# Two more activation tiles turned by transposed transfers, and the rows of the first block in another order

## The chip, the cores and the metric

The kernel runs on one core of a Trainium2 chip. The metric is device time in microseconds (us) of one execution; less is better. The core has five engines that run side by side, each with its own stream of instructions: TensorE (matrix products, and transposes by a product with the identity), VectorE (elementwise work and reductions), ScalarE (activations, copies out of the accumulators), GpSimd (POOL in the profile) and SyncE (SP), which mostly sends transfers between the device's memory and the on-chip buffer. A stream is worked off in order, and an instruction that waits holds everything behind it on its engine. Transfers of all queues are carried by the same sixteen DMA engines. Matrix products write to eight accumulator banks, which another engine has to empty.

## The reference

The reference computes a sum of three terms and all of its gradients: the input itself, a sequence branch A (short convolution, then a long convolution done through Fourier transforms, gated by the normed input) and a gated MLP, branch B. Only the MLP and the norm matter here. Sequence length S is 2048, width D 1024, hidden width F 3584; all in bf16.

```python
xn = _layernorm(x)                       # rows of D
gate = einsum("bsd,df->bsf", xn, W_gate)
up   = einsum("bsd,df->bsf", xn, W_up)
gate = gate * (gate > 0)
h = gate * up
out = x + A(xn, ...) + einsum("bsf,fd->bsd", h, W_down)
```

The gradient of h needs `grad_out` times `W_down` transposed, for the same rows and the same columns of F as gate and up. It is computed in the same pass.

## The kernel before

The sequence is cut into 16 tiles ("rows" below) of 128; a half is 8 rows. F is cut into 7 blocks of 512 columns. `hidden` (class `LnMlp`) runs over 14 steps: for each half, for each block. A step has its weights on chip: `wg` and `wu` (gate and up, 1024 x 512 each, in four transfers of 256 KB) and `wdT` (the down weights turned, four transposed transfers). For each of its 8 rows it does three products of eight 128 x 512 matmuls: `gate(s)`, `up(s)` (both with the turned activations `xnT` of the row) and `grad_row(s)` (with the turned output gradient `goT` of the row). ScalarE empties gate and gradient rows, VectorE masks and multiplies; the results go to device memory as `h_d` and `ug_d`.

The first step (`n == 0`, `ahead` in the code) is special, since nothing is on chip when the kernel starts. Its rows are normed while it runs. `layer_norm` is a generator: each `next(ln)`, or `chunk()`, which calls it up to three times, emits one more piece: sums on ScalarE, small steps on VectorE, the scaling by 1/std (line 991), which makes a tile ready. The input arrives in loads: load 4 holds tiles 4 and 5, load 5 tiles 6 and 7, later loads the rest.

`flip_xn(st)` (line 1131) turns a normed tile into `xnT`. For tiles 0 to 5 TensorE does it: eight 128 x 128 transposes into an accumulator bank (line 1141), then a copy out by VectorE, for tile 4 by ScalarE (line 1146). For tiles 6 and 7 SyncE sends a transposed transfer from the tile on chip (line 1134), without TensorE.

The order on TensorE in the first step is: rows 0 to 3 of gate and up, interleaved with the turning of tiles 0 to 3 (`first_rows`); gradient rows 0 and 1, with the turning of tiles 4 and 5 within row 1 (`grad(0)`, which calls `flip_ahead`); gate rows 4, 5, up rows 4, 5 (`gate_up(4)`); gradient rows 2, 3, 4, 5; gate rows 6, 7, up rows 6, 7; gradient rows 6, 7. Then the second step (`n == 1`) begins, with gate rows 0 and 1.

The order of transfers on SyncE's queue follows the program's order and priorities. `load_T` (line 1122) sends a turned gradient tile, `col_block` (line 1091) the gate or up weights of a step, `row_piece_T` (line 1116) a quarter of the down weights, `ln_load` (line 943) a load of the input. `issue_after(ins)` makes what is emitted inside it be placed after `ins`. A transfer takes one of eight completion semaphores in turn, and waits for the transfer that had it before. The gate weights of the second step go to a spare buffer; its up and down weights go to buffers that the first step's gate row 7 and up row 7 free. POOL's queue stores `h_d` and `ug_d` in the first step, and the normed tiles `xn_d`.

Of the kernel before, what the change touches and what calls it, by code (L numbers as in the profile page):

```python
# [17 lines left out]
P = 128  # L18
# [854 lines left out]
class LnMlp:  # L873
# [7 lines left out]
    def open_left(self):  # L881
        tc = self.tc
        self.per = tc.alloc_tile_pool(name="b_per", bufs=1, side="left")
        self.actp = tc.alloc_tile_pool(name="b_act", bufs=1, side="left")
        self.w2 = tc.alloc_tile_pool(name="b_w2", bufs=1, side="left")
        self.e2 = tc.alloc_tile_pool(name="b_e2", bufs=6, side="left")
        self.e1 = tc.alloc_tile_pool(name="b_e1", bufs=6, side="left")
        self.ps = tc.alloc_tile_pool(name="b_ps", bufs=8, space=bass.MemoryType.PSUM)
        self.ln_x, self.xn, self.todo, self.kept, self.hold, self.busy = [], [], [[]], [], False, False
        self.rstd = self.per.tile([P, self.ST], F32, name="rstd")  # L890
        self.ident = self.per.tile([P, P], BF16, name="ident")
        make_identity(self.nc, self.ident[:])
# [237 lines left out]

    def flip_xn(self, st):
        xT = self.act_tile("xnT", st)
        if st > 5:
            self.turned = self.nc.sync.dma_start_transpose(out=xT[:].rearrange("p (a b) -> p a b", b=P),
                                                           in_=self.xn[st])
            return xT
        h = self.DT // 2 if st < 3 else self.DT
        for k0 in range(0, self.DT, h):
            pst = self.ps.tile([P, self.DT, P], BF16, name="pst_x", tag="bps")
            for kt in range(k0, k0 + h):  # L1140
                self.pri.pin(self.nc.tensor.transpose(pst[:, kt, :], self.xn[st][:, kt * P:(kt + 1) * P],  # L1141
                                                      self.ident[:]), always=True)
            c = h // 2 if st == 0 and k0 == 0 else h
            for k in range(k0, k0 + h, c):
                copy = self.nc.scalar.copy if st == 4 else self.nc.vector.tensor_copy
                self.copied = copy(out=xT[:, k * P:(k + c) * P], in_=pst[:, k:k + c, :].rearrange("p a b -> p (a b)"))  # L1146
                if st < 5:
                    self.tc.keep_in_program_order(self.copied)
        return xT

    def warm(self, n):
# [9 lines left out]
    def hidden(self, first, goT, load, ln, tables, Wg, Wu, Wd, g, xn_d, h_d, ug_d):  # L1161


        nc, HS, N = self.nc, self.ST // 2, 2 * self.FB
        w, sets, spare = first, (0, 1, 2), 3
        self.g_nat, self.hs = [None] * self.ST, [None] * (self.ST // 2)
        xT, gT = [], goT
        for n in range(N):
            half, fb = divmod(n, self.FB)
            s0, cols, ahead = half * HS, slice(fb * 512, fb * 512 + 512), n == 0  # L1170
            swap, last = fb == self.FB - 1, n == N - 1
            if n and fb == 0:
                xT, gT = nxT, ngT
# [15 lines left out]
            def load_up():  # L1189
                if not last:  # L1190
                    nw[1] = self.col_block(Wu, nb, "wu", to[1])
# [21 lines left out]
            def up(s, mid=None, after={}, put=lambda *fs: [f() for f in fs], hold=False):  # L1213
                ps = self.ps_tile("ps_u")
                self.gemm8(ps, xT[s], wu, mid, after)

                def masked():
                    return self.pri.pin(nc.vector.scalar_tensor_tensor(  # L1218
                        out=ru[s][:, 1, :], in0=ru[s][:, 0, :], scalar=0.0, in1=ps[:], op0=ALU.is_gt, op1=ALU.mult),
                        always=hold)  # L1220

                def product():
                    ht = self.e1_tile("ht")
                    self.pri.pin(nc.vector.tensor_tensor(out=ht[:], in0=ru[s][:, 0, :], in1=ru[s][:, 1, :],
                                                         op=ALU.mult), always=hold)

                    def store(r=(s0 + s) * P, cols=cols, ht=ht):
                        queue = nc.gpsimd if n == 0 else nc.sync
                        self.stored = queue.dma_start(out=h_d[r:r + P, cols], in_=ht[:])
                        self.pri.pin(self.stored)  # L1230
                    self.defer(store)
                put(masked, product)

            def step(ns=1730):
                yield ns
                self.tick()
# [40 lines left out]
            def gate_up(sp):  # L1277
                end = sp == HS - 2
                if ahead:
                    flip(sp + 2)  # L1280
                for s in (sp, sp + 1):
                    gate(s)
                    yield from step(self.PACE[0])
                if end:
                    (load_up if ahead else load_gate)()
                for s in (sp, sp + 1):
                    up(s)
                    yield from step(self.PACE[1])
                if end and ahead:
                    for q in range(4):  # L1290
                        load_down(q)
                elif end:
                    load_up()
                if swap:
                    next_rows(sp)
# [68 lines left out]
            def grad(sp):  # L1364
                for s in (sp, sp + 1):
                    at = 3 if sp == 0 else 0
                    yield from grad_row(s, {at: lambda: flip_ahead(sp)} if ahead and s == sp + 1 else {})
                if swap:
                    next_grads(sp)
# [13 lines left out]
            for sp in range(0, HS, 2):  # L1383
                self.pri.now()
                while len(gT) < min(sp + 4, HS):
                    gT.append(self.load_T(g, len(gT), "goT", HS + len(gT)))
                if ahead or sp < HS - 4:
                    if not ahead:
                        load_down(sp // 2)
                        yield from gate_up(sp)  # L1390
                        if sp:
                            self.hold = False
                        elif fb:
                            self.busy = False
                    if not ahead or sp != 4:
                        yield from grad(sp)
                    if ahead and sp == 2:
                        yield from grad(4)
                elif sp == HS - 4:
                    yield from last_rows(sp)  # L1400
                if ahead:
                    with self.tc.issue_after(self.stored.ins):
                        if sp == 0:
                            load_gate()
                if ahead and sp in (2, 6):
                    with self.tc.issue_after(self.put.ins):
                        for put in self.kept[0:3] if sp == 2 else self.kept[3:7]:
                            put()
                if ahead and sp == 6:
                    with self.tc.issue_after(self.sent.ins):  # L1410
                        load(6)
                if ahead and sp + 4 < HS:
                    yield from gate_up(sp + 4)
                if n == 1 and sp < 4:
                    with self.tc.issue_after(self.stored.ins):
                        for i in ((7,), (8, 9))[sp // 2]:
                            load(i)
                if n == 1 and sp != 4:
                    chunk()
                if ahead and sp == 4:  # L1420
                    with self.tc.issue_after(self.ln_act.ins), self.tc.issue_after(self.ln_dve.ins):
                        tables()
# [358 lines left out]
def kernel(  # L1781
# [27 lines left out]
    x, g = A_q[0], grad_out[0]  # L1809
# [11 lines left out]
    b = LnMlp(tc, pri, S, D, F)  # L1821
    a = ABranch(tc, pri, S, D, A_k[0], A_v[0], g, A_shift_k, A_ssm_k, A_ssm_D, xn_d, y_d, sk_d[:], gks_d, gh_d, out_2[0],
                out_3[0], out_6)
# [12 lines left out]
    first.append(b.col_block(B_W_up, 0, "wu", 1, lambda: load(2)))  # L1836
    load(3)
    first.append(b.row_block_T(B_W_down, 0, "wdT", 2, lambda: load(4)))
    goT = [b.load_T(g, i, "goT", 8 + i) for i in range(2)]
    load(5)  # L1840
    goT += [b.load_T(g, i, "goT", 8 + i) for i in range(2, 4)]
    a.load_shift()
    ln = b.layer_norm(xn_d, a.tmp, "tmp", a.sm)
    def mlp():
# [52 lines left out]
```

## Time and profile before

| | |
|---|---|
| median of 3 runs | 1853.27 us (1853.05 to 1853.33) |
| profiled execution, its own time | 1853.43 us |
| span of the profile | 1851.7 us |
| ScalarE busy | 643.9 us (35%) |
| VectorE busy | 1115.3 us (60%) |
| granted TensorE clock | 1.00 |
| gradient rows 0, 1, with tiles 4, 5 turned | 23.34 to 27.68 us |
| gate row 6 starts | 41.61 us |
| the second step starts (gate row 0) | 51.98 us |

The span runs from the first to the last instruction; a run's time has about 1.7 us more around it. Times of single instructions are read from the timeline, counted from the start of the span; a row of the timeline merges equal instructions that follow each other (x16 is sixteen), with the start of the first and the time to the end of the last. A matmul of 512 columns is listed with 379 ns, but they are pipelined: starts are 0.216 us apart. "Idle before" in square brackets is how long the engine had nothing to do, and what ended that.

### The profile page before, as it was taken

How to read it: one execution, taken by the hardware profiler on the slowest of the kernel's cores; microseconds unless marked ns; L12 is line 12 of the kernel's file. 1: busy time of each engine (PE TensorE's matmuls, PEld its weight loads, DVE VectorE, ACT ScalarE, POOL GpSimd, SP SyncE). 2: the span in 40 equal slices, each digit the busy share in tenths (PEclk: the TensorE clock that was granted, in tenths of full speed). 3: DMA queues.
4: the chain of work that ended last, by engine and by line, in shares of the span. 5: the costliest groups of instructions: out<-in, count | busy, mean ns of one | idle time of the engine just before them, and what ended most of it. 6: DMA issues, size and time to landing. Idle time of an engine off the chain costs nothing.

```text
span 1851.7 us, 32066 instructions
## 1 busy us (share of the span) xinstructions
PE 1846.7 (100%) x13045; PEld 846.1 (46%) x13045; DVE 1115.3 (60%) x1632; ACT 643.9 (35%) x1212; POOL 35.0 (2%) x73
## 2 busy tenths in 40 slices
PE   9999999999999999999999999999999999999999
PEld 4444444444444444444444444444444544444444
DVE  6656797698789768585785667721212222466652
ACT  5644444445444454544544455320000000111100
POOL 2200000000000000000000000000000000000000
PEclk9999999999999999999999999999999999999999
DMA  9998679968767856549566544379999757799963
GB/s 254 277 221 184 150 174 226 213 174 204 175 168 195 248 144 177 145 118 254 154 169 147 150 120 148 118 224 258 259 236 249 180 145 165 175 212 204 212 156 74
DMA packets 746660, 345.17 MB, mean 186 GB/s; under 512 B 577944, under 2 KB 715152, under 8 KB 746512
## 3 DMA queue, kind: packets, MB, share of 16 engines
q1 hardware_dynamic: 732848, 311.39, 70.4%
q10 hardware_dynamic: 9504, 17.04, 2.9%
q0 software_dynamic: 4160, 14.68, 2.4%
q8 instruction: 102, 1.67, 0.4%
q14 instruction: 46, 0.38, 0.1%
HBM read 143.79 MB, written 103.83 MB: 134 GB/s over the span
## 4 chain that ended last, share of the span: by engine, by line
PE 99%; DMA 1%; DVE 0%; ACTq 0%; issue 0%; SPq 0%
PE ps_x L1747 21%; PE ps_w L1450 20%; PE ps_h L1098 11%; PE ps_u L1098 10%; PE ps_g L1098 10%; PE ps_o L1615 10%; PE ps_d L1450 9%; PE ps_c L83 4%; PE ps_d L1466 2%; PE ps_w L1466 1%; DMA wu<-in_B_W_up_dram 1%; PE ps_r L1649 0%; DMA ln_x<-in_A_q_dram 0%; PE pst_x L1141 0%; DVE rest L1653 0%; ACTq L943 0%
## 5 line engine op out<-in xcount | busy, mean ns | idle before, releaser
L1450 PE MATMUL ps_w<-ugs,xn_nat 128*128 128x512 bf16 x1728 | 381.1, 379 | 0.0
L87 ACT CAST arena<-ps_c 128x512 bf16<-128x512 f32 x576 | 293.9, 610 | 86.0 <-PE ps_c L83 85.2
L1098 PEld LDWEIGHTS <-xnT 128*128 128x128 bf16 x1792 | 171.6, 98 | 209.5 <-issue 6.1
L1450 PEld LDWEIGHTS <-xn_nat 128*128 128x128 bf16 x1728 | 165.3, 98 | 201.1 <-issue 6.7
L341 DVE STREAM_TRANSPOSE arena<-arena 128x1024 f32<-128x1024 f32 x96 | 180.4, 1934 | 126.5 <-ACT arena L87 108.5
L1098 PE MATMUL ps_u<-wu,xnT 128*128 128x512 bf16 x896 | 206.1, 379 | 0.4 <-DMA wu<-in_B_W_up_dram 0.3
L1098 PE MATMUL ps_g<-wg,xnT 128*128 128x512 bf16 x896 | 205.1, 379 | 0.2 <-DVE xnT L1146 0.2
L1098 PE MATMUL ps_h<-wdT,goT 128*128 128x512 bf16 x896 | 203.6, 379 | 0.0
L1747 PE MATMUL ps_x<-wgT,ggT 128*128 128x512 bf16 x896 | 198.6, 379 | 0.0
L1747 PE MATMUL ps_x<-wuT,guT 128*128 128x512 bf16 x896 | 198.6, 379 | 0.0
L1765 ACT ACTIVATE w<-xn,m 128x512 f32<-128x512 bf16 x32 | 24.3, 807 | 481.8 <-DVE m L1758 368.4
L1615 PE MATMUL ps_o<-wd,hT 128*128 128x512 bf16 (+1 forms) x896 | 187.6, 372 | 0.0
L1450 PE MATMUL ps_d<-g_nat,hs 128*128 128x512 bf16 x768 | 169.9, 379 | 0.0
L1747 PEld LDWEIGHTS <-guT 128*128 128x128 bf16 x896 | 87.7, 98 | 105.7
L1747 PEld LDWEIGHTS <-ggT 128*128 128x128 bf16 x896 | 87.7, 98 | 105.5
L1098 PEld LDWEIGHTS <-goT 128*128 128x128 bf16 x896 | 86.5, 98 | 104.2 <-issue 1.2
L1345 ACT CAST gh<-ps_h 128x512 bf16<-128x512 f32 x112 | 66.3, 592 | 194.0 <-PE ps_h L1098 186.9
L1615 PEld LDWEIGHTS <-hT 128*128 128x128 bf16 x896 | 87.7, 98 | 99.9
L1453 ACT CAST wi<-ps_w 128x512 bf16<-128x512 f32 x108 | 64.6, 598 | 189.5 <-PE ps_w L1450 149.5
L1218 DVE SCALAR_TENSOR_TENSOR ru<-ru,ps_u 128x512 bf16<-128x512 bf16 x112 | 76.3, 682 | 83.2 <-PE ps_u L1098 39.9
L1607 DVE TENSOR_TENSOR ya<-ya,xe 128x1024 bf16<-128x1024 bf16 x16 | 11.1, 692 | 173.3 <-DMA xe<-xn_d 173.3
L91 DVE TENSOR_TENSOR t<-arena 128x2048 bf16<-128x2048 bf16 x96 | 113.8, 1218 | 0.4
(143 smaller groups left out, 1405.8 us busy)
## 6 DMA issues: line engine op xcount, KB each, us to landing
ugs<-ug_d SPq DMA_DIRECT2D x112, 256.0 KB
ug_d<-ru SPq DMA_DIRECT2D x104, 256.0 KB
wg<-in_B_W_gate_dram SPq DMA_DIRECT2D x56, 256.0 KB
wu<-in_B_W_up_dram SPq DMA_DIRECT2D x56, 256.0 KB
hs<-h_d SPq DMA_DIRECT2D x56, 256.0 KB
out_dram<-wi SPq DMA_DIRECT2D x56, 256.0 KB
h_d<-ht SPq DMA_DIRECT2D x104, 128.0 KB
gt<-in_grad_out_dram SPq DMA_DIRECT2D x32, 256.0 KB
```

Of the source, the lines that this page charges most:

```text
L83: self.pri.pin(self.nc.tensor.matmul(out, lhsT=lhsT, rhs=rhs, start=start, stop=stop))
L87: self.pri.pin(self.nc.scalar.copy(out=out, in_=in_))
L91: self.pri.pin(self.nc.vector.tensor_tensor(out=out, in0=in0, in1=in1, op=op))
L341: self.pri.pin(self.nc.vector.transpose(out=df[:, c0:c0 + 32, :], in_=sf[:, c0:c0 + 32, :]))
L1098: self.pri.pin(self.nc.tensor.matmul(ps[:], lhsT=xT[:, kt * P:(kt + 1) * P], rhs=w(kt), start=(kt == 0), stop=(kt == self.DT - 1)), always ...
L1218: return self.pri.pin(nc.vector.scalar_tensor_tensor(out=ru[s][:, 1, :], in0=ru[s][:, 0, :], scalar=0.0, in1=ps[:], op0=ALU.is_gt, op1=ALU ...
L1345: self.pri.pin(nc.scalar.copy(out=gh[:], in_=ps[:]))
L1450: self.pri.pin(self.nc.tensor.matmul(ps[:], lhsT=lhsT(st), rhs=rhs(st), start=(st == 0), stop=(st == self.ST - 1)))
L1453: self.pri.pin(self.nc.scalar.copy(out=out, in_=ps[:]))
L1466: self.pri.pin(self.nc.tensor.matmul(ps[i][:], lhsT=lhsT(i, st), rhs=rhs(i, st), start=(st == 0), stop=(st == self.ST - 1)))
L1615: nc.tensor.matmul(ps, lhsT=hT[:, kt, :], rhs=self.wd[:, kt, oc], start=(kt == 0), stop=(kt == self.FT - 1))
L1747: nc.tensor.matmul(ps, lhsT=T[:, kt, :], rhs=W[:, kt, oc], start=(i == 0), stop=(i == n - 1))
```

## The change

Five edits, all of them in the first step.

Tiles 4 and 5 are turned by transposed transfers on SyncE too, like 6 and 7; the sixteen transposes on TensorE and the two copies go. The transfers are kept in a list, so that others can be placed after one of them: `turned[1]` is that of tile 5, `turned[3]` that of tile 7.

Gradient rows 2 and 3 come directly after rows 0 and 1, ahead of gate row 4. `grad(2)` calls `flip_ahead`, so tiles 6 and 7 are asked for there.

In `gate_up(4)` the order gate 4, gate 5, up 4, up 5 becomes gate 4, up 4, gate 5, up 5.

The turned gradient rows 2 and 3 are sent ahead of load 5 instead of behind it.

On SyncE, gradient rows 4 and 5 are sent behind the turned tile 5, and gradient rows 6 and 7, and the second step's gate weights, behind the turned tile 7. The queue's order was: gradient rows 0, 1, load 5, gradient rows 2, 3, the shift taps (`sk_b`), the gate weights, gradient rows 4 to 7, tiles 6, 7, the up weights. It becomes: gradient rows 0 to 3, load 5, the shift taps, tiles 4, 5, gradient rows 4, 5, tiles 6, 7, gradient rows 6, 7, the gate weights, the up weights.

On TensorE the order becomes: gradient rows 0 to 3; gate 4, up 4, gate 5, up 5; gradient rows 4, 5; and from gate row 6 on as before. On ScalarE and VectorE the copies go out of gradient rows and the masks follow the new order; on VectorE the products of gradient rows 2 and 3 now stand within the norm of tiles 6 and 7, and the mask of up row 4 behind it.

```diff
@@ flip_xn
-        if st > 5:
-            self.turned = self.nc.sync.dma_start_transpose(out=xT[:].rearrange("p (a b) -> p a b", b=P),
-                                                           in_=self.xn[st])
+        if st > 3:
+            self.turned.append(self.nc.sync.dma_start_transpose(out=xT[:].rearrange("p (a b) -> p a b", b=P),
+                                                                in_=self.xn[st]))
             return xT
...
-                copy = self.nc.scalar.copy if st == 4 else self.nc.vector.tensor_copy
-                self.copied = copy(out=xT[:, k * P:(k + c) * P], in_=pst[:, k:k + c, :].rearrange("p a b -> p (a b)"))
-                if st < 5:
-                    self.tc.keep_in_program_order(self.copied)
+                self.copied = self.nc.vector.tensor_copy(out=xT[:, k * P:(k + c) * P],
+                                                         in_=pst[:, k:k + c, :].rearrange("p a b -> p (a b)"))
+                self.tc.keep_in_program_order(self.copied)
@@ gate_up
-                for s in (sp, sp + 1):
-                    gate(s)
-                    yield from step(self.PACE[0])
-                if end:
-                    (load_up if ahead else load_gate)()
-                for s in (sp, sp + 1):
-                    up(s)
-                    yield from step(self.PACE[1])
+                todo = [(gate, sp), (gate, sp + 1), (up, sp), (up, sp + 1)]
+                if ahead and not end:
+                    todo[1:3] = todo[2:0:-1]
+                for k, (f, s) in enumerate(todo):
+                    if k == 2 and end:
+                        (load_up if ahead else load_gate)()
+                    f(s)
+                    yield from step(self.PACE[f is up])
@@ hidden, the loop over pairs of rows
                 while len(gT) < min(sp + 4, HS):
-                    gT.append(self.load_T(g, len(gT), "goT", HS + len(gT)))
+                    with self.tc.issue_after(self.turned[1 if sp < 4 else 3].ins):
+                        gT.append(self.load_T(g, len(gT), "goT", HS + len(gT)))
...
-                    if not ahead or sp != 4:
-                        yield from grad(sp)
-                    if ahead and sp == 2:
-                        yield from grad(4)
+                    for at in ((0, 2), (4,), (), (6,))[sp // 2] if ahead else (sp,):
+                        yield from grad(at)
...
-                    with self.tc.issue_after(self.stored.ins):
-                        if sp == 0:
+                    with self.tc.issue_after(self.turned[3].ins):
+                        if sp == 4:
                             load_gate()
@@ the kernel's start
-    goT = [b.load_T(g, i, "goT", 8 + i) for i in range(2)]
+    goT = [b.load_T(g, i, "goT", 8 + i) for i in range(4)]
     load(5)
-    goT += [b.load_T(g, i, "goT", 8 + i) for i in range(2, 4)]
```

More of the change, by code (lines that the diff above doesn't have):

```diff
@@ L888, in open_left @@
         self.ps = tc.alloc_tile_pool(name="b_ps", bufs=8, space=bass.MemoryType.PSUM)
-        self.ln_x, self.xn, self.todo, self.kept, self.hold, self.busy = [], [], [[]], [], False, False
+        self.ln_x, self.xn, self.todo, self.kept, self.turned, self.hold, self.busy = [], [], [[]], [], [], False, False
         self.rstd = self.per.tile([P, self.ST], F32, name="rstd")
```

## The prediction

> **What bounds the kernel now.** I read the page's busy times and chain first, because they say whether there is anything but TensorE to gain from.
>
> ```profile
> PE 1846.7 (100%) x13045; PEld 846.1 (46%) x13045; DVE 1115.3 (60%) x1632; ACT 643.9 (35%) x1212; POOL 35.0 (2%) x73
> PE 99%; DMA 1%; DVE 0%; ACTq 0%; issue 0%; SPq 0%
> ```
>
> TensorE is busy for 1846.7 of 1851.7 us and is 99% of the chain. So a part of TensorE's work that goes is worth its own time, and a new wait of TensorE costs its whole length. The waits of TensorE over the whole span come second:
>
> ```profile
> PE ps_warm L1157 <- POOL warm L1154: 1.5, 1, 1.5
> PE ps_u L1098 <- DMA wu<-in_B_W_up_dram: 0.3, 1, 0.3
> PE ps_g L1098 <- DVE xnT L1146: 0.2, 1, 0.2
> ```
>
> Nothing in the stretch that the change touches (23 to 62 us) is among them. Third, the timeline of that stretch on TensorE. It is the only place where the two programs' orders differ on TensorE; from gate row 6 of the first step on both have the same order.
>
> ```profile
> 23.34 2.75 PE L1098 MATMUL ps_h<-wdT,goT 128*128 128x512 bf16 x12
> 25.93 1.06 PE L1141 MATMUL pst_x<-ident,ln_x 128*128 128x128 bf16 x16
> 26.82 1.03 PE L1098 MATMUL ps_h<-wdT,goT 128*128 128x512 bf16 x4
> 27.68 3.62 PE L1098 MATMUL ps_g<-wg,xnT 128*128 128x512 bf16 x16
> ...
> 34.59 7.07 PE L1098 MATMUL ps_h<-wdT,goT 128*128 128x512 bf16 x32
> 41.61 3.63 PE L1098 MATMUL ps_g<-wg,xnT 128*128 128x512 bf16 x16
> ...
> 51.98 3.62 PE L1098 MATMUL ps_g<-wg,xnT 128*128 128x512 bf16 x16
> ```
>
> The starts give the pace: 27.68 to 34.59 is 32 matmuls, 0.216 us each, so a row of eight costs 1.73 us. 25.93 is the turning of tiles 4 and 5. Fourth, the same stretch on SyncE's queue, which sends everything in order, and the one sign of a late transposed transfer:
>
> ```profile
> 17.77 2.66 SPq L1122 DMA_TRANSPOSE goT<-in_grad_out_dram  x2
> 20.62 1.27 SPq L943 DMA_DIRECT2D ln_x<-in_A_q_dram  x1
> 21.93 3.92 SPq L1122 DMA_TRANSPOSE goT<-in_grad_out_dram  x2
> ...
> 26.52 2.48 SPq L1091 DMA_DIRECT2D wg<-in_B_W_gate_dram  x4
> 29.05 7.33 SPq L1122 DMA_TRANSPOSE goT<-in_grad_out_dram  x4
> 36.48 2.94 SPq L1134 DMA_TRANSPOSE xnT<-ln_x  x2
> 43.98 4.00 SPq L1091 DMA_DIRECT2D wu<-in_B_W_up_dram  x4
> 48.07 6.96 SPq L1116 DMA_TRANSPOSE wdT<-in_B_W_down_dram  x4
> ```
>
> ```profile
> 41.61 1.41 PEld L1098 LDWEIGHTS <-xnT 128*128 128x128 bf16 x8 [0.44 <-DMA xnT<-ln_x]
> ```
>
> Gate row 6 already starts on the landing of its transposed tile: it could have started at 34.59 + 32 x 0.216 = 41.50 and starts at 41.61. The trace's completion events (sixteen to a transfer) say when each landed: gradient rows 0 to 3 at 22.85, 23.94, 26.95, 28.88; load 5 (tiles 6, 7, between them) at 26.05; the shift taps 29.70; the four gate weights 30.78, 31.79, 33.17, 33.97; gradient rows 4 to 7 34.81, 36.61, 37.28, 39.70; turned tiles 6, 7 41.57, 43.20; up weights to 52.15; down weights to 57.48. The DMA share of 1.08 to 1.16 between 6 and 42 us says that transfers queue there.
>
> The last view is where tiles become ready: their scaling on VectorE.
>
> ```profile
> 24.71 0.88 DVE L991 TENSOR_SCALAR ln_x<-ln_x,rstd 128x1024 bf16<-128x1024 bf16 x2
> 34.62 0.88 DVE L991 TENSOR_SCALAR ln_x<-ln_x,rstd 128x1024 bf16<-128x1024 bf16 x2
> ```
>
> **The change part by part.** The profiled execution took 1853.43 us (span 1851.7, 1.7 around it), 0.16 above the median 1853.27. I work out a shift and set it on the median.
>
> *Sixteen transposes leave TensorE.* They hold it from 25.93 to 26.82: -0.89 us. Their copies (1.01 us on ScalarE, 0.68 on VectorE) ran beside matmuls; they are worth nothing directly.
>
> *Gradient rows 2, 3 come forward.* TensorE now runs rows 0 to 3 without a break, 23.34 + 32 x 0.216 = 30.25, and needs rows 2 and 3 at 26.8 and 28.5, against landings of 26.95 and 28.88 before. But load 5 (2.1 us between landings) no longer stands ahead of them: about 24.9 and 26.8, cover 1.7 us. Cost 0; without the cover 0.2 to 0.4.
>
> *Tile 4 by transposed transfer.* It is scaled at 25.19. Gate row 4 wants it at 30.25. Low end: the fastest transposed transfer in this trace landed 3.2 us after its issue (161.19 to 164.36): 28.4, no wait. High end: the same transfers stand ahead of it as ahead of the taps (29.70), and the widest spacing of transposed landings here is 2.4: 32.1, a wait of 1.9. I take 29.70 plus the spacing of gradient rows 0 and 1, 1.1, the nearest pair: 30.8, so +0.55. Tile 5 is sent some 1.3 us later, lands near 32.4, and is wanted only after up row 4, at 34.3: up row 4 going first is what hides it. Had gate row 5 kept its place, it would be wanted at 32.5.
>
> [...]
>
> *Tiles 6 and 7.* TensorE reaches gate row 6 at 41.50 - 0.89 + 0.55 = 41.16. Their chain starts with load 5, which now stands behind gradient rows 2, 3: 26.05 + 2 x 1.1 to 1.3, about 28.5. Before, ScalarE began its sums at 27.48 (after the copy of tile 4, now gone) and the first tile was scaled at 35.10, 7.6 us later. The built order puts two gradient products (0.68 each) into VectorE's part of that chain and takes one mask (0.68) out: 28.5 + 7.6 + 0.7 = 36.8. Sent then, at the head of an empty queue, tile 6 lands after 3.2 (fastest), 3.56 (gradient row 6, the nearest with little in front) to 5.1 us (tile 6 before, two in front): 40.0 to 41.9. I take 4.2, between them because three stores of the POOL queue are in flight: 41.0, so no wait. Gate row 6 then starts at 41.2 instead of 41.61: **-0.4**. Ends: 40.5 (every wait gone, -1.1) and 41.9 (+0.3); a load 5 landing 1 us later adds that.
>
> *What moves behind tiles 6, 7 on SyncE.* They hold the queue until scaled. Before, it stood idle from 39.4 to 43.98, which is where the two added transfers' 2.6 us go. Behind them wait gradient rows 6, 7 and the second step's gate weights: 36.8 + 4 x 1.3 = 42.0, then 2.48 for the gate weights: 44.5 instead of 29.0. They land within 5.45 (slowest gate row): 50.0. Wanted from 51.6 to 52.9: cover 1.6. Gradient rows 6, 7 land by 47, wanted at 48.1. The up weights wait for TensorE's gate row 7 anyhow (43.98); they go out 0.5 later, land by 52.7, wanted at 55.0 to 56.3. The down weights land by 58.0; the last quarter is wanted at 58.5 + 1.3 = 59.8. Cost 0, cover 1.6 to 2.3. If it is gone: six transfers of 256 KB come into a stretch at 248 to 353 GB/s, 4.5 to 6 us of work; at worst 57.5 + 5 = 62.5, a wait of 2.7.
>
> *POOL and the rest.* POOL's stores of rows 2 and 3 change places with h rows 4, 5; its busy time is 2%. The tables and later loads keep their order and have a whole step (41 us) of cover. Cost 0.
>
> Sum: -0.89 + 0.55 - 0.1 (the old wait at gate row 6) = -0.4; **1852.9 us**.
>
> **Rivals.**
> 1. *Load 5 decides.* Two transposed transfers now stand ahead of it. If it lands at 29.5 (a spacing of 1.7, as 23.21 to 28.88 was slow), tile 6 is scaled at 37.9 and with 5.1 us lands at 43.0: gate row 6 is 1.4 later than before: 1854.7. For it: gate row 6 was waiting before. Against: the queue is empty then.
> 2. *Full gain.* Tiles 4 and 6 land in 3.6 to 4.3 us and no wait is left: -1.0, **1852.3**. For it: gradient row 6's 3.56 us. Against: tiles 6, 7 took 5.1 and 5.4.
> 3. *The second step's weights are late.* The 2.7 us above on the unchanged -0.4: 1855.6. For it: DMA share 0.97 to 1.16 from 41.6 to 62. Against: no weight of this step was waited for before, and covers of 1.6 or more. It decides from a slip of 1.6 us; for slower by 0.2% it must reach 6.4.
> 4. *Tile 6 is stuck behind stores, the slower end.* The transposed transfer sent at 57.07 landed at 66.02, 8.95 us later, with POOL's tile stores in flight. So late, tile 6 lands at 45.8 and gate row 6 is 4.2 behind the old one: 1857.5, slower. It decides from 8.5 us. Against: at 57 four tile stores were leaving at once; at 37 POOL has gradient rows alone, 256 KB each, some 1 to 2 us apart.
>
> [...]
>
> **How the numbers follow.** 0.2%, 3.7 us, is about what a measurement of this kernel can tell from no change. Forecast (-0.8 to +0.4) 0.53; rival 1 0.18; rival 2 0.13; rival 3 0.12; rival 4 0.04. Range: 1852.1 (every wait gone, less the runs' spread of 0.2) to 1855.7 (rival 3 whole). Faster by 3.7 is excluded by 1.1 us of removable time: 0.02 for what I overlook. Slower: rival 4, and 0.04 for rivals 1 and 3 going together. Same 0.90.
>
> **What would show it.** No turning at 25.9; gradient rows 23.3 to 30.2 without a gap; a gap before gate row 4 of 0 to 1 us; gate row 6 at 41.2; the second step's first gate row at 51.6 and its gradient row at 58.5 with no wait on weights. A wait on wg, wu or wdT at 51 to 60, or gate row 6 after 41.9, makes it wrong.

## The result, and the profile after

The changed kernel takes 1861.16 us (median of six runs, 1859.58 to 1862.59), against 1853.16 us for the kernel before beside it (six runs, 1852.69 to 1854.36). The ratio is 1.0042, with a 95% interval of 1.0031 to 1.0053: slower by 8 us, outside the predicted range of 1852.1 to 1855.7. The profiled execution took 1861.37 us, 1.9 of it around the span.

The page's span, busy times and chain of the changed kernel:

```profile
span 1859.5 us, 31824 instructions
PE 1832.9 (99%) x12817; PEld 845.2 (45%) x13029; DVE 1115.4 (60%) x1631; ACT 642.9 (35%) x1211; POOL 34.9 (2%) x73
PE 96%; DMA 2%; issue 1%; DVE 0%; SPq 0%; ACT 0%; ACTq 0%; DVEq 0%
```

Part of what TensorE seems to have lost in busy time is not real: this trace lacks some matmul records (12817 matmuls against 13029 weight loads). Each missing one shows as a pause of 0.2 us put down to "issue", and these I leave out. What is real is the DMA share of 2% in the chain, which was 1%. The waits of TensorE over the whole span (what waited and on what: us in total, times, longest):

```profile
PE ps_h L1098 <- DMA wdT<-in_B_W_down_dram: 4.4, 2, 2.8
PE ps_g L1098 <- DMA xnT<-ln_x: 1.9, 1, 1.9
PE ps_g L1098 <- DMA wg<-in_B_W_gate_dram: 0.5, 1, 0.5
```

None of the three was there before. The same stretch on TensorE:

```profile
23.21 7.07 PE L1098 MATMUL ps_h<-wdT,goT 128*128 128x512 bf16 x32
32.21 1.90 PE L1098 MATMUL ps_g<-wg,xnT 128*128 128x512 bf16 x8 [1.93 <-DMA xnT<-ln_x]
...
42.58 3.62 PE L1098 MATMUL ps_g<-wg,xnT 128*128 128x512 bf16 x15
...
52.94 1.46 PE L1098 MATMUL ps_g<-wg,xnT 128*128 128x512 bf16 x6
54.95 2.32 PE L1098 MATMUL ps_g<-wg,xnT 128*128 128x512 bf16 x9 [0.55 <-DMA wg<-in_B_W_gate_dram]
57.10 3.62 PE L1098 MATMUL ps_u<-wu,xnT 128*128 128x512 bf16 x16
60.55 1.13 PE L1098 MATMUL ps_h<-wdT,goT 128*128 128x512 bf16 x4
64.51 0.59 PE L1098 MATMUL ps_h<-wdT,goT 128*128 128x512 bf16 x2 [2.83 <-DMA wdT<-in_B_W_down_dram]
66.71 3.90 PE L1098 MATMUL ps_h<-wdT,goT 128*128 128x512 bf16 x10 [1.61 <-DMA wdT<-in_B_W_down_dram]
70.45 3.40 PE L1098 MATMUL ps_g<-wg,xnT 128*128 128x512 bf16 x15
```

Gradient rows 0 to 3 run without a gap. Then gate row 4 waits for the turned tile 4; gate row 6 does not wait; the second step's first gate row waits for its weights; and its first gradient row waits twice, long, for quarters of the down weights. The last line is the row that stood at 62.34 before: 8.1 us later, which is all of the change in time (span +7.8, medians +8.0).

The row at 66.71 shows one thing more: ten matmuls in 3.90 us. At 0.216 a start they would take 2.3. The granted clock says why (stretch: its length, busy time of each engine with the number of instructions, then TensorE's granted clock, DMA share, GB/s):

```profile
61.30:66.54 5.24, 0.98 (x4) 0.29 (x3) 1.05 (x5) 0.32 (x1) 0.00 (x0) 1.00 1.14 291
66.54:69.96 3.42, 3.25 (x8) 1.16 (x8) 0.69 (x1) 0.59 (x1) 0.00 (x0) 0.50 1.06 270
```

After 5 us in which TensorE ran only a few matmuls, the clock was at 0.50 for 3.41 us, and matmuls started about 0.43 us apart instead of 0.216.

So the 8.1 us are: gate row 4 waits 2.09; sixteen transposes are gone, -0.89; the old wait at gate row 6 is gone, -0.12; the start is 0.13 earlier; the gate weights cost 0.71; the waits on the down weights 4.9; the half clock 1.6 (ten starts in 3.74 us instead of 2.16). Together +8.1. The waits are counted here from the time at which the next start was due, 0.216 us after the last; the view of waits counts from the listed end of the last matmul, 0.38 after its start, so its figures are smaller.

The queue that sent all this, SyncE:

```profile
25.35 5.41 SPq L1134 DMA_TRANSPOSE xnT<-ln_x  x2
30.81 2.87 SPq L1122 DMA_TRANSPOSE goT<-in_grad_out_dram  x2
37.76 2.66 SPq L1134 DMA_TRANSPOSE xnT<-ln_x  x2
40.47 3.29 SPq L1122 DMA_TRANSPOSE goT<-in_grad_out_dram  x2
43.80 2.36 SPq L1091 DMA_DIRECT2D wg<-in_B_W_gate_dram  x4
46.27 3.95 SPq L1091 DMA_DIRECT2D wu<-in_B_W_up_dram  x4
50.31 11.32 SPq L1116 DMA_TRANSPOSE wdT<-in_B_W_down_dram  x4
```

Two things are new. From 33.68 to 37.76 SyncE sends nothing: everything behind tiles 6 and 7 waits until they are scaled, and what was sent before has landed by 35.79. And the four down weights, 6.96 us of SyncE before, hold it for 11.32. By the completion events the gate weights landed 6.2 to 9.3 us after they were sent (54.90 the last, wanted from 52.94), the up weights at 55.64 to 58.14, and the down weights at 59.96, 61.05, 64.47 and 66.67. Before, the last of them landed at 57.48.

How full the DMA engines are, in the windows of the changed kernel:

```profile
32.00:36.00 4.00, 3.74 (x17) 1.78 (x19) 2.84 (x10) 4.00 (x9) 0.69 (x1) 1.00 1.07 213
36.00:40.00 4.00, 4.00 (x21) 1.77 (x19) 3.65 (x10) 0.82 (x2) 1.91 (x3) 1.00 0.63 170
44.00:48.00 4.00, 3.95 (x20) 1.79 (x19) 0.15 (x1) 1.19 (x2) 2.30 (x4) 1.00 1.16 210
52.00:56.00 4.00, 3.45 (x17) 1.46 (x15) 4.00 (x18) 2.53 (x4) 3.49 (x5) 1.00 1.07 379
```

The share (second figure from the end) is near 1 or above in every window from 28 to 64 us except 36 to 40, where it falls to 0.63 (1.20 before). In that window, SyncE's queue moved 152 KB, against 658 before.

### The profile page after: what moved, and what is told of

It reads as the page before. It is cut to its first block, busy times and chain, and to the rows that moved or that the text cites. A ratio compares the mean times of both kernels' runs of the same rounds, so it can differ in the third digit from the quotient of the medians.

```text
span 1859.5 us, 31824 instructions
## 1 busy us (share of the span) xinstructions
PE 1832.9 (99%) x12817; PEld 845.2 (45%) x13029; DVE 1115.4 (60%) x1631; ACT 642.9 (35%) x1211; POOL 34.9 (2%) x73
## 4 chain that ended last, share of the span: by engine, by line
PE 96%; DMA 2%; issue 1%; DVE 0%; SPq 0%; ACT 0%; ACTq 0%; DVEq 0%
PE ps_x L1745 21%; PE ps_w L1448 20%; PE ps_u L1098 10%; PE ps_g L1098 10%; PE ps_o L1613 10%; PE ps_h L1098 10%; PE ps_d L1448 9%; PE ps_c L83 4%; PE ps_d L1464 1%; PE ps_w L1464 1%; DMA wg<-in_B_W_gate_dram 0%; DMA ugs<-ug_d 0%; DMA wdT<-in_B_W_down_dram 0%; DMA xnT<-ln_x 0%; PE ps_r L1647 0%
## 5 line engine op out<-in xcount | busy, mean ns | idle before, releaser
L1448 PE MATMUL ps_w<-ugs,xn_nat 128*128 128x512 bf16 x1675 | 375.7, 379 | 4.4 <-issue 2.4
```

What stands on the lines that cost most here:

```text
L1448: self.pri.pin(self.nc.tensor.matmul(ps[:], lhsT=lhsT(st), rhs=rhs(st), start=(st == 0), stop=(st == self.ST - 1)))
```

## The experiments

Two theories came out of this. *Place*: the second step's weights are late because they stand behind tiles 6 and 7, which keep the queue empty until they are scaled. *Load*: they are late because two more transposed transfers go through DMA engines that were full. Each kernel is the changed one with one edit, unless it says otherwise. The first four ran against 1852.87 us for the kernel before (20 runs); the two after them (the order of gate rows, load 5) and the last two (tile 5 alone) against 1853.14 (22 runs); the four stores and the plain gradient rows against 1852.96 (14 runs). The changed kernel was not run beside them; it is compared by way of the kernel before.

### The gate weights ahead of tiles 6, 7

```diff
-                    with self.tc.issue_after(self.turned[3].ins):
-                        if sp == 4:
+                    with self.tc.issue_after(self.turned[1].ins):
+                        if sp == 0:
                             load_gate()
```

> The changed kernel, with the second step's gate weights sent directly behind the turned tile 5 instead of behind tile 7 and gradient rows 6, 7. Theory: the second step's weights are late because the gate weights wait on SyncE's queue behind tiles 6 and 7, which leave it empty from 33.7 to 37.8 us, and then meet POOL's stores of normed tiles. Then the waits of the second step (0.7 on gate weights, 4.9 on down weights, 1.6 at half pace after them) go, the wait at gate row 4 (2.1) stays, and the time is 1853.2 + 2.1 - 1.0 = 1854.3, 1853.8 to 1855. Rival: the two added transposed transfers overload the DMA engines wherever the weights stand; then a wait of 3 us or more on down weights is left, 1857 to 1861.

Measured: 1855.36 us (ratio 1.0011, 1.0002 to 1.0021), just above the forecast of 1853.8 to 1855. No wait on weights is left:

```profile
PE ps_g L1098 <- DMA xnT<-ln_x: 2.3, 1, 2.3
PE ps_h L1098 <- DMA goT<-in_grad_out_dram: 0.3, 1, 0.3
```

The gate weights landed by 37.89 and the last down weights at 60.78, before their first use at 62.1. With this order of rows, one place in the queue is worth 5.8 of the 8 us. What is left is the wait at gate row 4 and a small new one: gradient row 5, now behind the weights, landed at 41.76.

### Tiles 4, 5 turned by TensorE again

The old `flip_xn` is put back with `st > 5` and its copies, the gate weights stay behind tile 7, and the new order of rows stays.

```diff
-        if st > 3:
+        if st > 5:
...
-                    with self.tc.issue_after(self.turned[1 if sp < 4 else 3].ins):
+                    with self.tc.issue_after((self.copied if sp < 4 else self.turned[1]).ins):
...
-                    with self.tc.issue_after(self.turned[3].ins):
+                    with self.tc.issue_after(self.turned[1].ins):
```

Only two transposed transfers are left in the list, so `turned[1]` is that of tile 7 here.

> The changed kernel, with tiles 4 and 5 turned on TensorE again; the new order of rows and of the queue stays (gradient rows 6, 7 and the gate weights behind tile 7). Theory (place in the queue): the wait at gate row 4 goes, the 0.9 us of transposes come back, and the second step still waits 3 us or more for its down weights: 1857 to 1860. Rival (two transfers too many): the second step's waits go, 1853 to 1854.

Measured: 1861.08 us (ratio 1.0042, 1.0027 to 1.0057), the same as the changed kernel and above the 1857 to 1860 forecast, with the two added transfers gone.

```profile
PE ps_h L1098 <- DMA wdT<-in_B_W_down_dram: 5.1, 3, 3.9
```

SyncE sent nothing for longer here, from 28.83 to 35.56, and the gate weights left at 41.34. So the two added transfers are not needed for the loss: the new order of the queue can bring it without them. This execution also has no wait at gate row 4, and its time is no better for it.

### In the old kernel, the gate weights behind tile 7

```diff
-                    with self.tc.issue_after(self.stored.ins):
-                        if sp == 0:
+                    with self.tc.issue_after(self.turned.ins if sp == 4 else self.stored.ins):
+                        if sp == 4:
                             load_gate()
```

> The kernel before, with one edit: the second step's gate weights go behind the turned tile 7; gradient rows 4 to 7 stay ahead of tiles 6, 7. Theory: the queue does not run empty here, so the weights go out at about 39.4 instead of 43.8 and ahead of POOL's stores of normed tiles at 43.9; down weights land at most 1.5 us later than before, inside their cover: 1853.2 to 1854.2. Rival (the place behind tile 7 is enough by itself): waits of 3 us and more on down weights, 1856 to 1860.

Measured: 1853.52 us (ratio 1.0002, 0.9993 to 1.0012), no change. The gate weights left at 37.84 to 40.41, 11 to 12 us later than before, and in this stretch the only trace of it is

```profile
PE ps_h L1098 <- DMA wdT<-in_B_W_down_dram: 0.3, 1, 0.3
```

The last down weights landed at 60.37 instead of 57.48. The place behind tile 7 alone uses up the cover of 2.7 us that they had (they were wanted at 60.19 before). SyncE sends nothing here either, from 32.32 to 35.05 us, but gradient rows 4 to 7 have all gone out by then. In the changed kernel rows 6, 7 come behind the tiles, tile 6 is sent 2.7 us later than here (37.76 against 35.05), and the gate weights 6 us later (43.80 against 37.84). For that no cover is left. Which of the two counts for more was not taken apart.

### POOL's stores of tiles 1 to 3 sent later

```diff
-                if ahead and sp in (2, 6):
+                if ahead and sp == 6:
...
-                        for put in self.kept[0:3] if sp == 2 else self.kept[3:7]:
+                        for put in self.kept[0:7]:
```

> The changed kernel, with POOL's three stores of normed tiles 1 to 3 (768 KB, sent at 45.0 to 46.1) sent with those of tiles 4 to 7, some 12 us later. If these stores take the weights' share of the DMA engines, the gate weights land some 2 to 3 us earlier, the wait on down weights falls from 4.9 to 2 or less, and the half pace after it goes: 1855 to 1857. If the weights' late place in the queue alone sets their landing, the waits stay within 1 us of those of the changed kernel: 1860 to 1862.

Measured: 1859.11 us (ratio 1.0034, 1.0021 to 1.0047; five runs, 1857.37 to 1862.82), between the two forecasts. In the profiled execution the wait on the down weights fell from 4.4 to 1.9 by the waits' view, the clock stayed full, and the gate row behind them started at 65.27 instead of 70.45. Part of that is lost again: two new waits on ScalarE (1.3 us in all) stand at 77 to 81 us, and one of 0.8 on up weights at 147:

```profile
PE ps_h L1098 <- DMA wdT<-in_B_W_down_dram: 1.9, 1, 1.9
PE ps_u L1098 <- ACT ru L1210: 0.9, 1, 0.9
```

The first down weights held SyncE for 2.9 us instead of 4.7, and the last ones left at 57.74 instead of 59.58. So in this execution the load of POOL's stores counts too. By the median the gain is not clear of the spread.

### Gate rows 4, 5 ahead of up rows 4, 5 again

```diff
-                if ahead and not end:
-                    todo[1:3] = todo[2:0:-1]
```

> The change, but with the old order of its rows on TensorE: gate rows 4, 5 and then up rows 4, 5. Tile 5 landed at 33.78 us in the changed kernel, and gate row 5 would want it one row (1.73 us) after gate row 4's start at 32.21, at 33.94. Theory A (tile 5 comes out of the transposed transfers 1.6 us behind tile 4, so the row put between hides nothing once row 4 itself waits 2.1 us): no second wait over 0.2 us at gate row 5, the wait at the second step's down weights stays between 3.5 and 5.5 us, time within 1859.5 to 1862.5. Theory B (the order is what hides tile 5, as the prediction had it): a second wait of 0.5 to 2 us at gate row 5; by 42 us the program is that much later, and since the second step's weights are sent by other work, their wait shrinks by as much: time the same, but the wait is seen at 33.9 us.

Measured: 1860.1 us (ratio 1.0037, 1.0025 to 1.0049). The profiled execution says nothing on the order: its load 5 was sent 2 us earlier than in the changed kernel's, tile 4 landed at 28.91, tile 5 at 31.59, and neither row waited. But it shows something better (TensorE's timeline):

```profile
30.21 3.62 PE L1098 MATMUL ps_g<-wg,xnT 128*128 128x512 bf16 x16
...
58.32 1.21 PE L1098 MATMUL ps_h<-wdT,goT 128*128 128x512 bf16 x4
62.68 1.01 PE L1098 MATMUL ps_h<-wdT,goT 128*128 128x512 bf16 x2 [3.15 <-DMA wdT<-in_B_W_down_dram]
64.05 4.42 PE L1098 MATMUL ps_h<-wdT,goT 128*128 128x512 bf16 x10 [0.36 <-DMA wdT<-in_B_W_down_dram]
```

TensorE is 2.2 us earlier at the second step's gradient row (58.32 against 60.55), tile 6 and the gate weights were sent 2.4 and 2.6 us earlier, and the down weights were still not there until 64.01.

### Load 5 ahead of gradient rows 2, 3 again

```diff
-    goT = [b.load_T(g, i, "goT", 8 + i) for i in range(4)]
+    goT = [b.load_T(g, i, "goT", 8 + i) for i in range(2)]
     load(5)
+    goT += [b.load_T(g, i, "goT", 8 + i) for i in range(2, 4)]
```

> The change, with the load of input tiles 6, 7 again ahead of gradient rows 2, 3 on SyncE's queue. Theory A (tiles 6, 7 keep SyncE's queue empty until they are scaled, and that time comes from this load): the load lands 2 to 3.5 us earlier (26 to 27.5 instead of 29.6), ScalarE's sums start when they land or when ScalarE is free, tile 6 is scaled 1.5 to 2.5 us earlier, and the second step's weights land as much earlier: the wait at the down weights falls from 4.9 us to 2 to 3.5 and the clock stays full; gradient rows 2, 3 cost a new wait of 0 to 1 us; time 1856 to 1859.5. Theory B (the scaling of tile 6 is set by the engines' other work, not by the load): tile 6 is scaled within 0.5 us of 37.74 and the time stays at 1859.5 to 1862.

Measured: 1859.68 us (ratio 1.0036, 1.0022 to 1.0049; four runs at 1857.02, 1857.89, 1861.46 and 1862.01, the profiled one at 1861.46). In the profiled execution the first half of theory A came true: load 5 landed at 24.82 instead of 29.59 and tile 6 was sent at 34.01 instead of 37.76. The second half fell: the gate weights left 2.4 us earlier, at 41.43, but the wait grew.

```profile
34.01 4.67 SPq L1134 DMA_TRANSPOSE xnT<-ln_x  x2
38.73 2.65 SPq L1122 DMA_TRANSPOSE goT<-in_grad_out_dram  x2
41.43 2.32 SPq L1091 DMA_DIRECT2D wg<-in_B_W_gate_dram  x4
43.85 2.69 SPq L1091 DMA_DIRECT2D wu<-in_B_W_up_dram  x4
46.77 12.59 SPq L1116 DMA_TRANSPOSE wdT<-in_B_W_down_dram  x4
```

```profile
PE ps_h L1098 <- DMA wdT<-in_B_W_down_dram: 5.7, 3, 3.7
```

The four down weights were offered 3.5 us earlier than in the changed kernel, and the last landed only 1.0 earlier, at 65.65. Here the empty queue is nearly gone, and still the weights are late. Something other than the place in SyncE's queue holds the last of them in this execution.

### The last down weights against POOL's four stores

The landings of all kernels, side by side, show what. POOL sends the stores of normed tiles 4 to 7, 256 KB each, in one go at 56 to 62 us. In the changed kernel:

```profile
57.95 2.26 POOL L994 DMA_DIRECT2D xn_d<-ln_x  x4
```

| kernel | last down weights sent | landed | took | first of the four stores sent |
|---|---|---|---|---|
| before | 53.71 | 57.48 | 3.8 | 57.00 |
| old, gate weights behind tile 7 | 55.57 | 60.37 | 4.8 | 56.79 |
| gate weights ahead of tiles 6, 7 | 56.35 | 60.78 | 4.4 | 58.92 |
| stores of tiles 1 to 3 later | 57.74 | 63.08 | 5.3 | 57.89 (all seven) |
| tiles 4, 5 on TensorE | 56.94 | 65.34 | 8.4 | 56.66 |
| load 5 early | 57.43 | 65.65 | 8.2 | 56.33 |
| gate rows first | 57.98 | 64.01 | 6.0 | 55.94 |
| changed | 59.58 | 66.67 | 7.1 | 57.95 |

Sent ahead of the four stores, the last quarter takes 3.4 to 5.3 us (plain gradient rows, 4.6, and the two kernels with tile 5 alone, 3.4 and 4.3, included). Sent behind them, it takes 6.0 to 8.4. To test it, the four stores are left out there. Their part of `xn_d` is written in the second step with the data of later tiles, so this kernel leaves out part of the result:

```diff
             else:
                 put()
+            if 8 <= st < 12:
+                nc.gpsimd.dma_start(out=xn_d[(st - 4) * P:(st - 3) * P, :], in_=x)
             self.xn.append(x)
...
-                if ahead and sp in (2, 6):
+                if ahead and sp == 2:
...
-                        for put in self.kept[0:3] if sp == 2 else self.kept[3:7]:
+                        for put in self.kept[0:3]:
```

> The change, but POOL's four stores of normed tiles 4 to 7, sent at 57.9 to 59.7 us and landed at 62.4 to 65.6, are left out there; the rows of the array that they fill are written in the second step, beside the stores of tiles 8 to 11 and with those tiles' data, so that part of the result is left out. Theory A (the last down weights, sent at 58.0 and 59.6, land late because they share the DMA engines with these four stores): the first two down weights land as before (60 and 61), the last two at 62 to 64 instead of 64.5 and 66.7; the wait falls from 4.9 us to 1 to 2.5, the clock stays full, time 1855.5 to 1858. Theory B (the down weights are late by their place in SyncE's queue alone, the stores only fill gaps): the last one lands after 65.5, the wait stays over 4 us, time over 1859.5.

Measured: 1856.07 us (ratio 1.0015, 1.0005 to 1.0025; ten runs, 1854.28 to 1857.86), 5.1 less than the changed kernel. In the profiled execution, the slowest of the ten, the last two down weights were sent at 58.28 and 60.09, later than in the changed kernel, and landed 4.3 and 4.4 us after that, at 62.58 and 64.47:

```profile
PE ps_g L1100 <- DMA xnT<-ln_x: 2.6, 1, 2.6
PE ps_h L1100 <- DMA wdT<-in_B_W_down_dram: 0.5, 1, 0.5
```

Theory A holds, and the wait is below the 1 to 2.5 us that it allowed. (The wait of 2.6 is gate row 4's. It was followed by a half clock, against what was expected, and the second step's gradient row came 2 us later for it, at 62.52. That is part of why its wait is so short; the landings 4.3 and 4.4 us after the sending are the test.)

### Gradient rows 4 to 7 by plain transfers

```diff
-                        gT.append(self.load_T(g, len(gT), "goT", HS + len(gT)))
+                        gT.append((self.load_nat if ahead else self.load_T)(g, len(gT), "goT", HS + len(gT)))
```

> The change, but gradient rows 4 to 7 are loaded by plain transfers of the same 256 KB instead of transposed ones (their transposition is left out, so part of the result is). Theory A (the DMA engines are full from 20 to 66 us, and a transposed transfer takes 1.6 to 1.7 us of all sixteen where a plain one takes 0.8 to 0.95: the cost is time on the DMA engines, besides the empty queue at 36 us): four such transfers free about 3 us; the rows of gate weights go out 2 to 3 us earlier because SyncE is held less, the last down weights land 1.5 to 4 us earlier, the wait falls from 4.9 to 1 to 3.5 us, time 1855.5 to 1859. Theory B (only the queue that is empty while tiles 6, 7 are normed counts): tile 6 is sent at the same 37.8 within 0.5 us, and the wait stays over 4 us, time 1859.5 or more.

This kernel leaves out the turning of these rows, and with it part of the result.

Measured: 1859.26 us (ratio 1.003, 1.0017 to 1.0043), from runs at 1856.05, 1856.17, 1859.26, 1859.52 and 1862.08. The profiled one took 1856.17 and has no wait on weights at all:

```profile
PE ps_g L1098 <- DMA xnT<-ln_x: 2.0, 1, 2.0
```

(Gate row 4's, with a half clock behind it.) Its last down weights were sent at 57.27, ahead of the stores (59.96), and landed at 61.89. Tile 6 was sent at 38.04, as theory B had it, but the gate weights left 1.6 us earlier than in the changed kernel (42.19). The half clock has a part in this too: it put TensorE at the second step's gradient row at 61.86, 1.3 us later than in the changed kernel, and the stores left 2.0 later. That the slower three runs are the ones in which the last quarter did not pass the stores is an inference; they were not profiled. The median is just above what theory A allowed, so what the load of these rows is worth stays open.

### Tile 5 alone, and the weights early

Two kernels without either cause. TensorE turns tile 4 again (`st > 4`), and gate weights and gradient rows 4, 5 are sent behind tile 5; in the second kernel the two gradient rows go ahead of the weights (`sp == 2`).

```diff
-        if st > 3:
+        if st > 4:
...
-                    with self.tc.issue_after(self.turned[1 if sp < 4 else 3].ins):
+                    with self.tc.issue_after(self.turned[0 if sp < 4 else 2].ins):
...
-                    with self.tc.issue_after(self.turned[3].ins):
-                        if sp == 4:
+                    with self.tc.issue_after(self.turned[0].ins):
+                        if sp == 0:
```

> The change, but tile 4 is turned by TensorE again (eight transposes, 0.45 us, instead of sixteen), only tiles 5, 6, 7 go by transposed transfer, and the second step's gate weights and gradient rows 4, 5 are sent behind tile 5, ahead of tiles 6, 7. Theory A (two causes: tile 4 has no row of cover for a transposed transfer, and the second step's weights must not stand behind tiles 6, 7): no wait at gate row 4, tile 5 lands before up row 4 ends at about 34.2, gradient row 5 waits 0 to 0.5 us as its transfer shares the queue with tiles 6, 7, no wait on weights: 0.45 us gained by the transposes, 0.1 by the old wait: 0.5 us faster to 0.2 slower than before, 1852.3 to 1853.1. Theory B (any transposed transfer more in this stretch makes the later ones late): a wait of 1 us or more at gradient row 5, gate row 6 or the weights, 1854 or more.

> As the kernel with tile 5 alone and the weights early, but gradient rows 4, 5 ahead of the four gate weights on SyncE's queue. Theory A: gradient row 5 then lands at 36 to 38 us instead of about 40, so no wait there; the gate weights go out by 37 and land by 43, 9 us ahead of their use; the same 0.5 us faster to 0.1 slower than before, and 0 to 0.5 us faster than the kernel with the weights first. Theory B (the eight transfers between tile 5 and tile 6 hold SyncE past tile 6's scaling at 37.7, whatever their order): tile 6 is sent after 38.5, gate row 6 waits 0.5 us or more in both, no difference between the two over 0.3 us.

Measured: 1852.88 us (1.0001, 0.9992 to 1.001) and 1853.0 us (1.0001, 0.9992 to 1.001). Both are level with the kernel before; 0.45 us cannot be told from nothing here. The first one's profiled execution took 1855.33: gate row 6 started 0.9 late, at 41.86, and gradient row 7 waited.

```profile
PE ps_g L1098 <- ACT gh L1344: 0.7, 1, 0.7
PE ps_h L1098 <- DMA goT<-in_grad_out_dram: 0.3, 1, 0.3
```

The first line names ScalarE, but tile 6, sent at 37.96, landed at 41.81, just ahead of the start. Gradient row 7's transfer, behind the tiles, took 7.8 us to 51.19. In the second kernel's profiled execution (1852.93) tile 6 was sent at 36.50, and only gate rows 6 and 7 wait a little for their tiles:

```profile
PE ps_g L1098 <- DMA xnT<-ln_x: 0.5, 2, 0.3
```

Tile 4 on TensorE takes away the wait at gate row 4 in both, and no weight is waited for in either. Where the two differ, in gradient row 5's landing (38.97 and 33.15), neither was late. No version was found that beats the kernel before by more than can be measured.

## Why the prediction was wrong, step by step

*What bounds the kernel, and the transposes* (-0.89). Right: gradient rows 0 to 3 run from 23.21 to 30.1 without a gap.

*Gradient rows 2, 3.* Right at a cost of 0: they landed at 25.09 and 26.98 (24.9 and 26.8 forecast).

*Tile 4.* Right in kind, too small: 0.55 taken, 2.09 measured, just over the high end of 1.9. It was sent at 25.35 and landed at 32.16; its issue alone held SyncE for 4.06 us, with load 5 and the shift taps ahead of it in the queue until 29.95. (That the backlog is what held the issue is an inference.) It is also the least steady term: in the traces tile 4 landed between 28.91 and 33.15, and gate row 4 waited between nothing and 2.6 us.

From 20 to 66 us of the changed kernel, the packets of transposed transfers took 1.65 us of all sixteen engines for each 256 KB, those of the weights 0.81 (the sum of packet times by size, over 16, over the bytes): twice the time for the same bytes.

*Tile 5.* Right that it is not waited for (33.78). That the order of up row 4 hides it was not shown: in the one run without that order it came early.

*Tiles 6, 7.* Gate row 6 does not wait, but by luck. Load 5 landed at 29.59, not 28.5, and tile 6 was scaled at 37.7, not 36.8: that is rival 1's condition. It then landed 3.4 us after it was sent, not 4.2, at 41.16; the two errors nearly cancel against the 41.0 forecast. The wait at gate row 4 gave it more time still; gate row 6 started at 42.58, past the 41.9 that the prediction named as its own refutation.

*What moves behind tiles 6, 7 on SyncE.* This is the step that failed. The prediction gave it a cost of 0; it measured 7.2 of the 8 us (0.71 on the gate weights, 4.9 on the down weights, 1.6 at half clock). The gate weights were sent 1.7 to 1.8 us later than forecast (43.80 to 46.17 instead of 42.0 to 44.5), which the delay of TensorE itself, 1.3, nearly covers. The sentence "they land within 5.45" did not hold: they took 6.2 to 9.3. It took the slowest gate row from 28.5 us; the same trace had an up weight sent at 44.44, beside POOL's three stores, that took 6.01. In the changed kernel two gradient rows, the same three stores and eight weights were sent between 40 and 50 us, with the DMA share at 1.04 to 1.16. From there on the slip grew instead of being absorbed: the first down weights' issue held SyncE for 4.7 us and the second's for 2.8, the last two left at 58.00 and 59.58, with POOL's four stores, and landed 6.5 and 7.1 us later, where without those stores it was 4.3 and 4.4. The bound "at worst 62.5, a wait of 2.7" spread the bytes evenly; what came was 66.67. Of the 9.2 us by which the last quarter landed later than before, 5.9 are its later sending (59.58 against 53.71) and 3.3 its slower landing (7.1 us against 3.8), where the slip had carried it into another queue's burst.

The prediction had that row in its hand. Rival 4 quotes a transposed transfer sent at 57.07 that landed 8.95 us later with the four stores in flight, and used it to price tile 6 at 37 us, where there are none. The last down weights were wanted 1 to 3 us after those same stores leave; the row belonged to rival 3, from the moment that transfer slips past 57 us.

*The half clock* (1.6 us). The forecast has no term for it; in the trace of the kernel before, the one clock record stands at 1.00. In the changed kernel the clock was at 0.50 for 3.41 us, which cost 1.6; at gate row 4 it cost 1.7 in the two kernels that have it there (the four stores left out, plain gradient rows). It fell on rival 3, which named the mechanism that came, but with a price of 2.7 us and without this term.

*The sum.* Adding waits along TensorE was also not sound here. In the three kernels whose traces have no wait or almost none at gate row 4 (tiles 4, 5 on TensorE, gate rows first, load 5 early) the time is within 1.5 us of the changed kernel's. TensorE arrives earlier at the second step's gradient row (58.55, 58.32 and 58.23 against 60.55), but goes on with the landing of the last down weights (65.34, 64.01 and 65.65 against 66.67); and in all three the half clock lasts 6.83 us instead of 3.41.

## What to carry to other kernels

Where the DMA engines are as full as here (a share of 1.06 to 1.26 in each window from 48 to 64 us), a transfer that moves back in a queue can arrive later by more than it is sent later (5.9 us became 9.2 for the last down weights): what other queues send at that moment counts as well (with POOL's four stores the last quarter took 7.1 us, without them 4.4), and so, by an inference, does what is queued ahead of it. For each moved transfer, list the bursts of the other queues between its old and its new time, and ask what it costs if it falls behind one. Be wary of urgent transfers behind one that must wait for data on its queue (here the tiles being normed): with the new order of rows the gate weights' place was worth 5.8 of 8 us. In the old kernel the same place cost nothing, since the cover of 2.7 us was enough; so work out the cover first.

## What the runs showed of the hardware

The half clock, as the traces have it: in the changed kernel it lasted 3.413 us, from 66.54 us, which is 61.44 us, 18 times 3.413, after the trace's first clock record; with POOL's four stores left out it lasted 3.41 us (34.48 to 37.89), with load 5 early 6.83 (63.91 to 70.74). Two kernels with nearly the same wait at gate row 4 (2.6 and 2.3 us), the one with POOL's four stores left out and then the one with the gate weights ahead, differ in how long TensorE was busy in the window of 3.41 us just before (first line of each; the second is the window behind it):

```profile
31.07:34.48 3.41, 1.29 (x6) 0.60 (x7) 1.65 (x4) 3.41 (x8) 0.00 (x0) 1.00 1.08 275
34.48:37.89 3.41, 3.19 (x8) 1.22 (x8) 2.20 (x11) 2.64 (x6) 1.57 (x3) 0.50 0.63 155
```

```profile
30.69:34.10 3.41, 1.46 (x7) 0.70 (x8) 1.65 (x4) 3.41 (x8) 0.00 (x0) 1.00 1.05 290
34.10:37.50 3.40, 3.35 (x17) 1.57 (x16) 2.37 (x11) 2.45 (x6) 1.75 (x3) 1.00 1.12 230
```

Busy 1.29 us of 3.41, the next window is at half; busy 1.46, it is not. Three more windows at full clock had a half one behind them: 0.59 us busy in the changed kernel (63.13 to 66.54), 1.38 with plain gradient rows, 1.42 from 58.91 with tiles 4, 5 on TensorE. One with 1.48 in the changed kernel (29.00 to 32.41) had not. The ends of matmuls are modelled, so 1.42 and 1.46 can hardly be told apart, and no threshold is shown. In these executions, the waits of 2.6 us (four stores left out) and 2.0 (plain gradient rows) at gate row 4 cost 1.7 us more by a half clock; those of 1.9 (the changed kernel) and 2.3 (gate weights ahead) cost nothing more.

The other surprise is how long the sending itself can take. In the traces of both kernels up to 70 us, a transposed transfer of 256 KB held SyncE for 1.23 to 1.25 us at the least; in the changed kernel the first down weights, sent at 50.31 with weights ahead of them still in flight (the last gate and up weights landed at 54.90 and 58.14), held it for 4.70. What limits it is not shown. The plain transfers of gate and up weights, of the same size, took 0.37 to 1.81.
